# A third w_out block moved out of the big weight transfer, by GpSimd transfers of three shares

## The chip, the core and the metric

The kernel runs on one NeuronCore of a Trainium2 chip. The core has five engines with their own instruction queues: TensorE (PE) multiplies matrices, VectorE (DVE), ScalarE (ACT) and GpSimd (POOL) work on vectors, and SyncE (SP) here only issues DMA transfers. Data comes from HBM into SBUF, a memory of 128 partitions, over 16 DMA engines. The metric is the device time of one execution in microseconds: the kernel before takes 680.47 us (median of three runs, 680.44 to 680.62).

## What is computed

One decoding step of a layer: attention with a key/value cache, and a gated MLP whose output gates the attention's. Cut to what matters:

```python
# x [8,1,512]; k_cache, v_cache [8 batches, 8 kv heads, 4096 keys, 128]; wq [512,4096]; wo [4096,512]
# w_in [512, 1792]; w_out [896, 512]; all float32
xn = layernorm(x)
q  = (xn @ wq) in 32 heads; 4 query heads share one kv head
s  = softmax(q @ k.T / sqrt(128)) @ v, heads joined, @ wo
z  = gelu(xn @ w_in); z1, z2 = z[:896], layernorm(z[896:])
g  = silu((z1 * (w_sp * z2 + b_sp)) @ w_out)
out = x + s * g
```

Almost all bytes are the two caches, 134 MB each. Every byte is used once.

## The kernel before

**Slots.** SBUF holds a ring of three slots of 64 KB per partition (8 MB each). `slot()` takes the next one; a transfer into it waits until the last readers of its old contents are done. The first slot gets wq, the second (`mlp_slot`) all that the MLP needs, the third the first half of K of head 0; from then on K and V halves of the heads follow one another through the ring, each an 8 MB transfer over all 128 partitions, issued by SP in program order (L325 in `load_k`, L332 in `load_v`). At the end come wo and the last V in smaller pieces (L359 to L363), so that little work is left when the last piece lands.

**The MLP's slot.** `w_mlp` is one transfer over 128 partitions (L96): w_in, five of the seven 128-row blocks of w_out, and `side` (x and two scalars). Blocks 1 and 3 of w_out (`MOVED = 2`) are not in it. They lie in `w_ex`, a tile of 64 partitions by 7 units of 512 columns, cleared by a memset on POOL (L98) and then filled by four transfers from SP (L99 and L100). `LANES` lists them: partition group, number of shares of four partitions, first unit, number of units. The four bring 5, 5, 3 and 3 shares; the host lays each array out with a fifth row behind every four (`QUAD + 1`), so that the share stays the leading count of the transfer.

**The MLP's order.** `project_q(0)`, `project_q(1)` and `mlp()` run on PE before the first scores (L347 to L349). In `mlp()`, after gelu and the layer norm, the gated hidden values stand in `u_sb`, 32 rows for each of four column groups. Two transposes make `hT` (L204 to L207) for the five blocks that stayed. For the moved ones `spread` (cleared on POOL, L210) takes the hidden columns in the order in which `w_ex` holds the rows of w_out, by copies that `lane_runs()` lists (L211 to L214); seven transposes give `te`, one copy `hE` (L215 to L219). Then five block matmuls (L224) and seven unit matmuls with 64 rows each (L228) add up in `pw`. The slot is free for V of head 0 when they are done. A scheduler places the instructions of each engine; an instruction that is ready early, such as a memset on POOL, can come ahead of others that stand before it in the program.

**Setup.** POOL also makes the identity (L104), clears `xnT`, `qz`, `pick` and others, and computes the power in the layer norm of x (L149), which all PE work waits for.

Of the kernel before, what the change touches and what calls it, by code (L numbers as in the profile page):

```python
# [8 lines left out]
F32 = mybir.dt.float32  # L9
# [4 lines left out]
P = 128  # L14
B, D = 8, 512
HKV, REP, S, DH = 8, 4, 4096, 128
NK = D // P
G = 4
J = S // (G * P)
R = 32  # L20
FH = 896
FQ = 256
NB = FH // P
MOVED = 2
QUAD = 4
UNITS = 7
LANES = [(0, 5, 0, 6), (1, 5, 0, 5), (1, 3, 5, 2), (0, 3, 6, 1)]
EPS = 1e-5
GELU_C = 0.7978845608028654
HALF = B // 2  # L30
# [7 lines left out]
AHEAD = FOLDED + 2  # L38


def lane_runs():
    f = 0
    for e, k, u, n in LANES:
        m = k * QUAD
        at, end = f, f + n * m
        while at < end:
            g = at // P
            stop = min(end, (g + 1) * P)
            unit, lo = divmod(at - f, m)
            if lo or stop - at < m:  # L50
                whole, size = 1, min(m - lo, stop - at)
            else:
                whole, size = (stop - at) // m, m
            yield g, at - g * P, u + unit, whole, e * R + lo, size
            at += whole * size
        f = end


@with_exitstack
def tile_gqa_gmlp_decode(ctx: ExitStack, tc: tile.TileContext, x, kT, v, wq, wo, w_mlp, w_ex0, w_ex1, w_ex2, w_ex3, out, gate, stored):  # L60
    nc = tc.nc
    head = ctx.enter_context(tc.tile_pool(name="head", bufs=1))
    l = head.tile([P, HKV], F32, name="l")
# [6 lines left out]
    small = ctx.enter_context(tc.tile_pool(name="small", bufs=2))  # L70
# [3 lines left out]
    def slot():  # L74
        return ring.tile([P, SLOT], F32, name="slot")
# [5 lines left out]
    mlp_slot = slot()  # L81
    n_in, n_out = NK * 2 * FH, (NB - MOVED) * D
    n_mlp = n_in + n_out + P
    w_in_sb = mlp_slot[:, :n_in].rearrange("p (k n) -> p k n", k=NK)
    w_out_sb = mlp_slot[:, n_in:n_in + n_out].rearrange("p (j d) -> p j d", j=NB - MOVED)
    side_sb = mlp_slot[:, n_in + n_out:n_mlp]
    spare = [n_mlp]

    def from_slot(rows, n):
        lo = spare[0]  # L90
        spare[0] = lo + n
        return mlp_slot[:rows, lo:lo + n]
# [1 line left out]
    x_sb = from_slot(B, D)  # L94
    nc.sync.dma_start(x_sb, x)
    nc.sync.dma_start(mlp_slot[:, :n_mlp], w_mlp)  # L96
    w_ex = from_slot(2 * R, UNITS * D).rearrange("p (u d) -> p u d", u=UNITS)
    nc.gpsimd.memset(w_ex, 0.0)  # L98
    for (e, k, u, n), src in zip(LANES, (w_ex0, w_ex1, w_ex2, w_ex3)):  # L99
        nc.sync.dma_start(w_ex[e * R:e * R + k * QUAD, u:u + n], src[:, :QUAD])  # L100


    ident = const.tile([P, P], F32, name="ident")
# [30 lines left out]
    def scratch(shape, name):  # L134
        t = ps.tile([P, 512], F32, name="scr")
        n = 1
        for s in shape[1:]:
            n *= s
        return t[:shape[0], :n]
# [18 lines left out]
    def mlp():  # L158
        zu = work.tile([P, 2, 2, FQ], F32, name="zu", tag="p")
        z, u_sb = zu[:, 0], zu[:, 1]  # L160
        rest = work.tile([P, 2 * D], F32, name="rest", tag="pT")
        hT, y_sb = rest[:, :2 * P], rest[:, D:]
        hT = hT.rearrange("p (a s) -> p a s", a=2)
        pz = scratch([P, 2 * FQ], "pz")
        nc.vector.memset(pz, 0.0)
        pz_v = pz.rearrange("p (a f) -> p a f", a=2)
        w_in_v = w_in_sb.rearrange("p k (a f) -> p k a f", a=2)
        for k in range(NK):
            for g in range(G):
                lo = g * FQ  # L170
                n = min(FQ, FH - lo)
                nc.tensor.matmul(pz_v[R * g:R * (g + 1), :, :n], xnT[:, k, :],
                                 w_in_v[:, k, :, lo:lo + n], start=(k == 0), stop=(k == NK - 1))
        zf, uf = z.rearrange("p a f -> p (a f)"), u_sb.rearrange("p a f -> p (a f)")
        nc.vector.tensor_copy(zf, pz)
        nc.vector.tensor_mul(uf, zf, zf)
        nc.vector.tensor_scalar(uf, uf, 0.044715, 1.0, op0=ALU.mult, op1=ALU.add)
        nc.vector.tensor_mul(uf, uf, zf)
        nc.scalar.activation(uf, uf, AF.Tanh, scale=GELU_C)
        nc.vector.tensor_scalar(uf, uf, 1.0, 0.5, op0=ALU.add, op1=ALU.mult)  # L180
        nc.vector.tensor_mul(zf, uf, zf)

        def mean(src, name, eps=0.0):
            part_sum = small.tile([P, 1], F32, name="part_sum")
            nc.vector.tensor_reduce(part_sum, src, op=ALU.add, axis=AX.X)  # L185
            pm = scratch([P, 1], "pm")
            nc.tensor.matmul(pm, same_all, part_sum, start=True, stop=True)  # L187
            t = small.tile([P, 1], F32, name=name)
            nc.vector.tensor_scalar(t, pm, 1.0 / FH, eps, op0=ALU.mult, op1=ALU.add)
            return t  # L190

        z1, z2 = z[:, 0, :], z[:, 1, :]
        mu = mean(z2, "mu")
        nc.vector.tensor_scalar(z2, z2, mu, None, op0=ALU.subtract)
        nc.vector.tensor_mul(u_sb[:, 0, :], z2, z2)
        nc.vector.memset(u_sb[(G - 1) * R:, 0, FH - (G - 1) * FQ:], 0.0)
        var = mean(u_sb[:, 0, :], "var", EPS)
        rs = small.tile([P, 1], F32, name="rs")
        nc.gpsimd.tensor_tensor(rs, var, neg_half, op=ALU.pow)
        nc.vector.tensor_scalar(z2, z2, rs, None, op0=ALU.mult)  # L200
        nc.vector.tensor_scalar(z2, z2, side_sb[:, W:W + 1], side_sb[:, W + 1:W + 2],
                                op0=ALU.mult, op1=ALU.add)
        nc.vector.tensor_mul(u_sb[:, 1, :], z2, z1)
        for a in range(2):  # L204
            th = scratch([P, P], "th")
            nc.tensor.transpose(th, u_sb[:, 1, a * P:(a + 1) * P], ident)  # L206
            nc.vector.tensor_copy(hT[:, a, :], th)  # L207
        wide = MOVED * R
        spread = from_slot(wide, UNITS * 2 * R).rearrange("p (u s) -> p u s", u=UNITS)
        nc.gpsimd.memset(spread, 0.0)  # L210
        for g, f, u, n, lo, m in lane_runs():  # L211
            rows = slice(R * g, R * (g + 1))
            nc.vector.tensor_copy(spread[rows, u:u + n, lo:lo + m],
                                  u_sb[rows, 1, P + f:P + f + n * m].rearrange("p (u s) -> p u s", u=n))  # L214
        te = scratch([2 * R, UNITS * wide], "te")  # L215
        for i in range(UNITS):
            nc.tensor.transpose(te[:, i * wide:(i + 1) * wide], spread[:, i, :], ident[:wide, :wide])  # L217
        hE = from_slot(2 * R, UNITS * wide)
        nc.vector.tensor_copy(hE, te)  # L219
        pw = scratch([P, D], "pw")  # L220
        kept = [j for j in range(NB) if j % 2 == 0 or j // 2 >= MOVED]
        for i, j in enumerate(kept):
            g, a = divmod(j, 2)
            nc.tensor.matmul(pw[R * g:R * (g + 1), :], hT[:, a, R * g:R * (g + 1)], w_out_sb[:, i, :],  # L224
                             start=(a == 0), stop=False)
        for i in range(UNITS):
            lo = wide * (i % 2)
            nc.tensor.matmul(pw[lo:lo + wide, :], hE[:, i * wide:(i + 1) * wide], w_ex[:, i, :],  # L228
                             start=False, stop=(i >= UNITS - 2))
        nc.vector.tensor_copy(y_sb, pw)  # L230
        py = scratch([P, W], "py")
        for g in range(G):
            for a in range(2):
                nc.tensor.matmul(py[R * g:R * (g + 1), :], pick[:, a, :],
                                 y_sb[:, (2 * g + a) * W:(2 * g + a + 1) * W], start=(a == 0), stop=(a == 1))
        nc.vector.tensor_copy(x_out, side_sb[:, :W])
        e = work.tile([P, W], F32, name="e", tag="o_all")
        nc.vector.tensor_scalar(e, py, -1.0, 87.0, op0=ALU.mult, op1=ALU.min)
        nc.scalar.activation(e, e, AF.Exp)
        nc.vector.tensor_scalar(e, e, 1.0, None, op0=ALU.add)  # L240
        nc.vector.reciprocal(e, e)
        nc.vector.tensor_mul(gate, py, e)
# [57 lines left out]
    turn = [0]  # L300
# [34 lines left out]
    part = sc[:, 0, :]  # L335
# [11 lines left out]
    project_q(0)  # L347
    project_q(1)
    mlp()  # L349
    for h in range(HKV):  # L350
        for half in range(2):
# [3 lines left out]
        for half in range(2):  # L355
# [11 lines left out]
            n = 2 if last else HALF  # L367
# [28 lines left out]
    for a in range(2):  # L396
        for g in range(G):
            c = (2 * g + a) * W
            nc.tensor.matmul(acc[R * g:R * g + OUT_ROWS, :], pick[:, a, :OUT_ROWS], part_f[:, c:c + W],
                             start=False, stop=False)  # L400
# [54 lines left out]
```

## Time and profile before

| | |
|---|---|
| median of three runs | 680.47 us (680.44 to 680.62) |
| the profiled execution | 680.28 us |
| its span, first to last instruction | 678.8 us |
| PE, DVE, ACT, POOL busy | 51%, 12%, 2%, 1% |
| DMA | 291 MB, mean 429 GB/s |
| memset of w_ex (L98) | 3.08 us, from 0.88 us |
| x landed (L146 starts) | 22.66 us |
| MLP's last matmul, V of head 0 issued | 63.98 us |
| last piece of wo landed (L391 starts) | 676.25 us |

The profiled execution has 1.48 us around its span. The page gives for each engine its busy time, in forty equal slices the busy tenths of the engines and of the 16 DMA engines together, the DMA queues with their packets (q1 is SP's, q10 the store's from ACT, q8 and q14 are listed as instruction queues), and the chain of waits that ended last. A packet is what one DMA engine moves in one piece, at most 64 KB. Each transfer also leaves one record of 4 bytes per engine that it used, its completion. The time of one packet can be read from a stretch that holds only that packet: its share of 16 engines, times the length of the stretch, times 16.

### The profile page before, as it was taken

What the parts mean: (1) busy time and instruction counts of PE and PEld (TensorE: products, weight loads), DVE (VectorE), ACT (ScalarE), POOL (GpSimd) and SP (SyncE); (2) the same over time, 40 slices, a digit from 0 to 9 for tenths busy, and PEclk for the clock granted to TensorE, in tenths of its full rate; (3) what the DMA queues carried; (4) which work ended last, traced back from release to release, by engine and by line L of the source; (5) the groups of instructions that cost most, each with busy time, mean ns of one, the idle gap of its engine ahead of it and who ended that gap; (6) DMA issues with size and microseconds to landing.
All of it is one profiled execution on the core that took longest, in us unless ns stands there. A gap on an engine that the chain in (4) does not pass through costs nothing.

```text
span 678.8 us, 5218 instructions
## 1 busy us (share of the span) xinstructions
PE 344.0 (51%) x2415; PEld 92.5 (14%) x2415; DVE 83.4 (12%) x159; ACT 13.4 (2%) x27; POOL 7.9 (1%) x17
## 2 busy tenths in 40 slices
PE   0448744446655454555554344555544345555567
PEld 0112211111111011111111011111111011111111
DVE  1143021102110021101100021101101021100221
ACT  0010000000000000000000000000000000000000
POOL 3000000000000000000000000000000000000000
PEclk9987866787776568777666778877666787876679
DMA  9999999999999999999999999999999999999997
GB/s 386 453 441 430 430 433 430 433 430 433 434 433 430 433 433 430 433 441 440 434 433 430 436 436 434 440 434 433 430 433 430 433 433 434 430 436 433 419 427 315
DMA packets 6741, 291.16 MB, mean 429 GB/s; under 512 B 888, under 2 KB 888, under 8 KB 1688
## 3 DMA queue, kind: packets, MB, share of 16 engines
q1 hardware_dynamic: 6576, 290.80, 99.1%
q8 instruction: 19, 0.31, 0.2%
q10 hardware_dynamic: 144, 0.03, 0.0%
q14 instruction: 2, 0.02, 0.0%
HBM read 290.80 MB, written 0.03 MB: 428 GB/s over the span
## 4 chain that ended last, share of the span: by engine, by line
DMA 79%; PE 16%; issue 4%; DVE 0%; SPq 0%; POOLq 0%; POOL 0%
DMA slot<-in_kT 36%; DMA slot<-in_v 33%; PE sc L269 7%; PE o_ps L310 7%; DMA slot<-in_wo 7%; DMA slot<-in_x 3%; PE scr L224 1%; PE scr L228 1%; SPq L332 0%; PE scr L217 0%; DVE st L146 0%; POOLq L449 0%; POOL rstd L149 0%; PE scr L206 0%; PE acc L391 0%
## 5 line engine op out<-in xcount | busy, mean ns | idle before, releaser
L269 PE MATMUL sc<-slot,qz 128*32 128x512 f32 x1024 | 145.4, 731 | 131.2 <-DMA slot<-in_kT 131.2
L310 PE MATMUL o_ps<-slot,pT 128*16 128x512 f32 x1024 | 148.2, 743 | 110.0 <-DMA slot<-in_v 110.0
L269 PEld LDWEIGHTS sc<-slot,qz 128*32 128x32 f32 x1024 | 38.1, 131 | 232.0 <-issue 149.4
L310 PEld LDWEIGHTS o_ps<-slot,pT 128*16 128x16 f32 x1024 | 32.9, 114 | 211.0 <-issue 151.5
L274 DVE TENSOR_REDUCE nm<-sc 128x1 f32<-128x1024 f32 x8 | 9.8, 1225 | 273.7 <-PE sc L269 273.7
L313 DVE TENSOR_TENSOR o_all<-o_ps,diag 128x512 f32<-128x512 f32 x17 | 11.8, 692 | 244.8 <-PE o_ps L310 244.8
L276 ACT ACTIVATE p<-sc,nm 128x1024 f32<-128x1024 f32 x8 | 8.9, 1114 | 551.8 <-DVE nm L274 551.8
L320 PE MATMUL po_ps<-fold,o_sb 128*128 128x16 f32 x30 | 6.0, 274 | 26.8 <-DVE o_sb L315 26.8
L315 DVE TENSOR_REDUCE o_sb<-o_all 128x128 f32<-128x512 f32 x17 | 17.8, 1047 | 0.6
L153 PE MATMUL scr<-ident,slot 8*128 8x8 f32 x4 | 0.6, 254 | 25.0 <-DVE slot L150 25.0
L320 PEld LDWEIGHTS po_ps<-fold,o_sb 128*128 128x128 f32 x30 | 4.5, 189 | 40.6 <-DVE o_sb L315 40.6
L296 DVE STREAM_TRANSPOSE pT<-p 128x1024 f32<-128x1024 f32 x8 | 10.0, 1246 | 0.3
L249 PE MATMUL scr<-slot,xnT 128*32 128x512 f32 x64 | 8.9, 708 | 0.3 <-issue 0.3
L344 PE MATMUL sc<-slot,oT 128*8 128x512 f32 (+1 forms) x60 | 8.4, 565 | 1.1 <-DMA slot<-in_wo 1.0
L279 PE MATMUL scr<-ident,nm 128*1 128x128 f32 x8 | 2.2, 270 | 10.8 <-DVE nm L274 10.8
L292 PE MATMUL scr<-wl,same 128*128 128x1 f32 x16 | 3.6, 297 | 6.5 <-DVE wl L290 6.5
L294 DVE TENSOR_SCALAR p<-p,w,wl 128x1024 f32<-128x1024 f32 x8 | 6.5, 813 | 0.3
L224 PE MATMUL scr<-slot,rest 128*32 128x512 f32 x10 | 5.4, 1044 | 0.0
L187 PE MATMUL scr<-part_sum,same 128*128 128x1 f32 x4 | 1.1, 348 | 8.4 <-DVE part_sum L185 8.4
L285 PE MATMUL scr<-ident,full 1*128 1x1 f32 x8 | 1.8, 220 | 5.0 <-DVE full L283 5.0
L292 PEld LDWEIGHTS scr<-wl,same 128*128 128x128 f32 x16 | 3.2, 249 | 7.0 <-PE scr L285 7.0
L153 PEld LDWEIGHTS scr<-ident,slot 8*128 8x128 f32 x4 | 0.5, 208 | 25.0 <-DVE slot L150 25.0
(94 smaller groups left out, 69.0 us busy)
## 6 DMA issues: line engine op xcount, KB each, us to landing
slot<-in_v SPq DMA_DIRECT2D x2, 4096.0 KB, 28.7
slot<-in_w_mlp SPq DMA_DIRECT2D x1, 4928.0 KB, 32.7
slot<-in_wo SPq DMA_DIRECT2D x1, 2048.0 KB
slot<-in_wo SPq DMA_DIRECT2D x1, 1536.0 KB
slot<-in_wo SPq DMA_DIRECT2D x1, 1280.0 KB, 37.9
slot<-in_wo SPq DMA_DIRECT2D x1, 1024.0 KB
slot<-in_wo SPq DMA_DIRECT2D x4, 256.0 KB, 18.7
slot<-in_wo SPq DMA_DIRECT2D x1, 768.0 KB
```

The source lines that it names most:

```text
L224: nc.tensor.matmul(pw[R * g:R * (g + 1), :], hT[:, a, R * g:R * (g + 1)], w_out_sb[:, i, :], start=(a == 0), stop=False)
L249: nc.tensor.matmul(pq[R * g:R * (g + 1), :], xnT[:, k, :], wq_sb[:, k, lo:lo + REP * DH], start=(k == 0), stop=(k == NK - 1))
L269: nc.tensor.matmul(sc[R * g:R * (g + 1), c, :], qz[:, h, b * R:(b + 1) * R], k_sb[:, i, c, g, :], start=(b == 0), stop=(b == B - 1))
L274: nc.vector.tensor_reduce(m, sc, op=ALU.max, axis=AX.XY, negate=True)
L276: nc.scalar.activation(p, sc.rearrange("p c s -> p (c s)"), AF.Exp, bias=m, accum_out=l[:, h:h + 1])
L292: nc.tensor.matmul(tot, same_all, wl, start=True, stop=True)
L296: nc.vector.transpose(pT.rearrange("p j b g r -> p j g b r"), p.rearrange("p (j g b r) -> p j g b r", j=J, g=G, b=B))
L310: nc.tensor.matmul(of[R * c:R * c + G * REP, :], pT[:, j, b0 + i], v_sb[:, i, j], start=(j < rows), stop=(j >= J - rows))
L313: nc.vector.tensor_mul(o_all, o, diag[:, :, None].to_broadcast([P, G, DH]))
L315: nc.vector.tensor_reduce(o_sb, o_all.rearrange("p g d -> p d g"), op=ALU.add, axis=AX.X)
L320: nc.tensor.matmul(po[:, b0 * REP:(b0 + n) * REP], o_sb, f.rearrange("p i r -> p (i r)"), start=True, stop=True)
L344: nc.tensor.matmul(part[R * q:R * q + B, i * n:(i + 1) * n], oT[:, h, r, :], wo_sb[:, m, i * n:(i + 1) * n], start=(m < REP), stop=(cuts = ...
```

## The change

`MOVED` becomes 3: block 5 of w_out leaves `w_mlp` too, which then holds four blocks. `w_ex` grows from 64 to 128 partitions. The four SP transfers keep their sizes and places. Three more bring the third block: 12 partitions from 84 for units 0 to 4, 12 from 116 for units 0 to 4, and 12 from 84 for unit 6, each of three shares of four partitions. GpSimd issues them (`nc.gpsimd.dma_start`), and ahead of each it issues a transfer of 16 bytes into each of 13 partitions of a small tile `turn`, whose contents nobody reads and of which two buffers exist. `spread` and `hE` become wider: a unit now has 128 rows of w_out, of which the unused ones are zero. `hT` needs only one transpose, as the blocks that stay are the even ones. A fixed list `RUNS` takes the place of `lane_runs()`: eight copies into `spread` instead of six. The host side builds the seven arrays from the same list.

```diff
--- before.py
+++ after.py
@@ -21,10 +21,14 @@
 FH = 896
 FQ = 256
 NB = FH // P
-MOVED = 2
+MOVED = 3
 QUAD = 4
 UNITS = 7
-LANES = [(0, 5, 0, 6), (1, 5, 0, 5), (1, 3, 5, 2), (0, 3, 6, 1)]
+LANES = [(0, 20, 0, 6), (32, 20, 0, 5), (32, 12, 5, 2), (0, 12, 6, 1)]
+HIGH = [(84, 12, 0, 5), (116, 12, 0, 5), (84, 12, 6, 1)]
+RUNS = [(0, 0, 0, 0, 3, 0, 2, 20), (0, 0, 120, 5, 1, 0, 1, 8), (1, 1, 0, 5, 1, 8, 1, 12),
+        (1, 1, 12, 5, 1, 32, 1, 12), (0, 1, 24, 3, 2, 0, 2, 20), (0, 1, 104, 6, 1, 0, 2, 12),
+        (1, 2, 0, 0, 5, 84, 2, 12), (1, 2, 120, 6, 1, 84, 1, 8)]
 EPS = 1e-5
 GELU_C = 0.7978845608028654
 HALF = B // 2
@@ -38,26 +42,8 @@
 AHEAD = FOLDED + 2
 
 
-def lane_runs():
-    f = 0
-    for e, k, u, n in LANES:
-        m = k * QUAD
-        at, end = f, f + n * m
-        while at < end:
-            g = at // P
-            stop = min(end, (g + 1) * P)
-            unit, lo = divmod(at - f, m)
-            if lo or stop - at < m:
-                whole, size = 1, min(m - lo, stop - at)
-            else:
-                whole, size = (stop - at) // m, m
-            yield g, at - g * P, u + unit, whole, e * R + lo, size
-            at += whole * size
-        f = end
-
-
 @with_exitstack
-def tile_gqa_gmlp_decode(ctx: ExitStack, tc: tile.TileContext, x, kT, v, wq, wo, w_mlp, w_ex0, w_ex1, w_ex2, w_ex3, out, gate, stored):
+def tile_gqa_gmlp_decode(ctx: ExitStack, tc: tile.TileContext, x, kT, v, wq, wo, w_mlp, w_ex0, w_ex1, w_ex2, w_ex3, w_hi0, w_hi1, w_hi2, out, gate, stored):
     nc = tc.nc
     head = ctx.enter_context(tc.tile_pool(name="head", bufs=1))
     l = head.tile([P, HKV], F32, name="l")
@@ -94,10 +80,14 @@
     x_sb = from_slot(B, D)
     nc.sync.dma_start(x_sb, x)
     nc.sync.dma_start(mlp_slot[:, :n_mlp], w_mlp)
-    w_ex = from_slot(2 * R, UNITS * D).rearrange("p (u d) -> p u d", u=UNITS)
+    w_ex = from_slot(P, UNITS * D).rearrange("p (u d) -> p u d", u=UNITS)
     nc.gpsimd.memset(w_ex, 0.0)
-    for (e, k, u, n), src in zip(LANES, (w_ex0, w_ex1, w_ex2, w_ex3)):
-        nc.sync.dma_start(w_ex[e * R:e * R + k * QUAD, u:u + n], src[:, :QUAD])
+    for (p, m, u, n), src in zip(LANES, (w_ex0, w_ex1, w_ex2, w_ex3)):
+        nc.sync.dma_start(w_ex[p:p + m, u:u + n], src[:, :QUAD])
+    for (p, m, u, n), src in zip(HIGH, (w_hi0, w_hi1, w_hi2)):
+        turn = small.tile([13, QUAD], F32, name="turn")
+        nc.gpsimd.dma_start(turn, w_mlp[:13, :QUAD])
+        nc.gpsimd.dma_start(w_ex[p:p + m, u:u + n], src[:, :QUAD])
 
 
     ident = const.tile([P, P], F32, name="ident")
@@ -159,8 +149,7 @@
         zu = work.tile([P, 2, 2, FQ], F32, name="zu", tag="p")
         z, u_sb = zu[:, 0], zu[:, 1]
         rest = work.tile([P, 2 * D], F32, name="rest", tag="pT")
-        hT, y_sb = rest[:, :2 * P], rest[:, D:]
-        hT = hT.rearrange("p (a s) -> p a s", a=2)
+        hT, y_sb = rest[:, :P], rest[:, D:]
         pz = scratch([P, 2 * FQ], "pz")
         nc.vector.memset(pz, 0.0)
         pz_v = pz.rearrange("p (a f) -> p a f", a=2)
@@ -201,28 +190,31 @@
         nc.vector.tensor_scalar(z2, z2, side_sb[:, W:W + 1], side_sb[:, W + 1:W + 2],
                                 op0=ALU.mult, op1=ALU.add)
         nc.vector.tensor_mul(u_sb[:, 1, :], z2, z1)
-        for a in range(2):
-            th = scratch([P, P], "th")
-            nc.tensor.transpose(th, u_sb[:, 1, a * P:(a + 1) * P], ident)
-            nc.vector.tensor_copy(hT[:, a, :], th)
-        wide = MOVED * R
-        spread = from_slot(wide, UNITS * 2 * R).rearrange("p (u s) -> p u s", u=UNITS)
+        th = scratch([P, P], "th")
+        nc.tensor.transpose(th, u_sb[:, 1, :P], ident)
+        nc.vector.tensor_copy(hT, th)
+        wide = 2 * R
+        spread = from_slot(wide, UNITS * P).rearrange("p (u s) -> p u s", u=UNITS)
         nc.gpsimd.memset(spread, 0.0)
-        for g, f, u, n, lo, m in lane_runs():
-            rows = slice(R * g, R * (g + 1))
-            nc.vector.tensor_copy(spread[rows, u:u + n, lo:lo + m],
-                                  u_sb[rows, 1, P + f:P + f + n * m].rearrange("p (u s) -> p u s", u=n))
-        te = scratch([2 * R, UNITS * wide], "te")
+        for place, g, f, u, n, p, segs, m in RUNS:
+            dst = spread[place * R:(place + 1) * R, u:u + n]
+            src = u_sb[g * R:(g + 1) * R, 1, P + f:P + f + n * segs * m]
+            if segs == 2:
+                half = p // (2 * R) * 2 * R
+                dst = dst[:, :, half:half + 2 * R].rearrange("p u (e s) -> p u e s", e=2)
+                nc.vector.tensor_copy(dst[:, :, :, p - half:p - half + m],
+                                      src.rearrange("p (u e s) -> p u e s", u=n, e=2))
+            else:
+                nc.vector.tensor_copy(dst[:, :, p:p + m], src.rearrange("p (u s) -> p u s", u=n))
+        te = scratch([P, UNITS * wide], "te")
         for i in range(UNITS):
             nc.tensor.transpose(te[:, i * wide:(i + 1) * wide], spread[:, i, :], ident[:wide, :wide])
-        hE = from_slot(2 * R, UNITS * wide)
+        hE = from_slot(P, UNITS * wide)
         nc.vector.tensor_copy(hE, te)
         pw = scratch([P, D], "pw")
-        kept = [j for j in range(NB) if j % 2 == 0 or j // 2 >= MOVED]
-        for i, j in enumerate(kept):
-            g, a = divmod(j, 2)
-            nc.tensor.matmul(pw[R * g:R * (g + 1), :], hT[:, a, R * g:R * (g + 1)], w_out_sb[:, i, :],
-                             start=(a == 0), stop=False)
+        for g in range(G):
+            nc.tensor.matmul(pw[R * g:R * (g + 1), :], hT[:, R * g:R * (g + 1)], w_out_sb[:, g, :],
+                             start=True, stop=False)
         for i in range(UNITS):
             lo = wide * (i % 2)
             nc.tensor.matmul(pw[lo:lo + wide, :], hE[:, i * wide:(i + 1) * wide], w_ex[:, i, :],
@@ -421,13 +413,18 @@
     vv = c(A_v_cache).reshape(2, HALF, HKV, P, J, G, DH)
     w_out = c(B_w_out).reshape(NB, P, D)
     moved = list(range(1, 2 * MOVED, 2))
-    rows = w_out[moved].reshape(MOVED * P, D)
-    w_ex, f = {}, 0
-    for i, (e, m, u, n) in enumerate(LANES):
-        t = np.zeros((m, QUAD + 1, n, D), np.float32)
-        t[:, :QUAD] = rows[f:f + n * m * QUAD].reshape(n, m, QUAD, D).transpose(1, 2, 0, 3)
-        w_ex[f"w_ex{i}"] = t.reshape(m, QUAD + 1, n * D)
-        f += n * m * QUAD
+    rows = w_out[moved]
+    extra = np.zeros((P, UNITS, D), np.float32)
+    for _, g, f, u, n, p, segs, m in RUNS:
+        part = rows[g, f:f + n * segs * m].reshape(n, segs, m, D)
+        for t in range(segs):
+            extra[p + t * R:p + t * R + m, u:u + n] = part[:, t].transpose(1, 0, 2)
+    w_ex = {}
+    for name, lanes in (("w_ex", LANES), ("w_hi", HIGH)):
+        for i, (p, m, u, n) in enumerate(lanes):
+            t = np.zeros((m // QUAD, QUAD + 1, n * D), np.float32)
+            t[:, :QUAD] = extra[p:p + m, u:u + n].reshape(m // QUAD, QUAD, n * D)
+            w_ex[f"{name}{i}"] = t
     arrays = {
         "x": x,
         "kT": c(k.transpose(2, 0, 7, 1, 5, 3, 6, 4)).reshape(HKV, 2, P, SLOT),
```

## The prediction

> **What bounds the kernel now.** I read the page first: engine shares, DMA row, queues, chain of waits.
>
> ```profile
> span 678.8 us, 5218 instructions
> ...
> DMA  9999999999999999999999999999999999999997
> ...
> q1 hardware_dynamic: 6576, 290.80, 99.1%
> q8 instruction: 19, 0.31, 0.2%
> ...
> q14 instruction: 2, 0.02, 0.0%
> ...
> DMA 79%; PE 16%; issue 4%; DVE 0%; SPq 0%; POOLq 0%; POOL 0%
> ```
>
> The 16 DMA engines are busy in every slice, and nearly all of it is q1, the queue that SP feeds. The 16% of PE in the chain is not a loss: a matmul group releases a slot, SP issues the next load behind transfers that are still running, and the chain runs through the matmuls while the DMA engines work. The chain in order of time shows that, and stretches of the trace (length, then five engines, clock, DMA share, GB/s) show that no engine runs dry until the tail:
>
> ```profile
> 60.32 3.59 PE scr L228 x14
> 63.98 32.31 DMA slot<-in_v
> ...
> 665.08 11.13 DMA slot<-in_wo
> 676.25 0.46 PE acc L391 x16
> ```
>
> ```profile
> 62.00:72.00 10.00, 9.22 (x88) 2.97 (x84) 1.89 (x5) 0.26 (x1) 0.00 (x0) 1.00 1.00 433
> 154.00:628.00 474.00, 240.27 (x1648) 62.72 (x1648) 47.90 (x79) 8.45 (x18) 0.00 (x0) 0.72 1.00 433
> 672.20:674.00 1.80, 1.33 (x14) 0.23 (x14) 0.00 (x0) 0.00 (x0) 0.00 (x0) 1.00 0.84 330
> 674.80:675.60 0.80, 0.69 (x37) 0.47 (x32) 0.29 (x1) 0.00 (x0) 0.00 (x0) 1.00 0.44 172
> 676.00:678.80 2.80, 0.45 (x20) 0.24 (x16) 0.45 (x2) 0.00 (x0) 0.00 (x0) 0.83 0.08 18
> ```
>
> The tail is the heart of it. A share of 0.84 is 13 engines of 16 (0.81, and a little overlap of records); 0.44 is 7. So three engines are done by 672.2, six more between 674.0 and 674.8, and the last seven near 676.1, when the last piece of wo lets L391 go. The seven most loaded engines set the end; the early three have some 3.9 us to spare. What counts is the load of each engine, not the sum.
>
> Where the unevenness comes from shows in the completions (records under 512 B) of the first K load, queued right behind w_ex, counted in 52.7 to 53.3, 56.2 to 56.6 and 56.8 to 57.4 us:
>
> ```profile
> DMA packets 22, 0.72 MB, mean 1202 GB/s; under 512 B 11, under 2 KB 11, under 8 KB 11
> ...
> DMA packets 4, 0.13 MB, mean 328 GB/s; under 512 B 2, under 2 KB 2, under 8 KB 2
> ...
> DMA packets 6, 0.20 MB, mean 328 GB/s; under 512 B 3, under 2 KB 3, under 8 KB 3
> ```
>
> Eleven engines are done first, two 3.4 us later, three 4.4 us later: the w_ex transfers of 5, 5, 3 and 3 shares all start on the same engine. Had each gone on where the last one stopped, 5+5+3+3=16 would have given every engine one share.
>
> **The change, part by part.** Prices of single transfers come from stretches that hold one packet alone, where its time is the share times the stretch times 16. Before this are 16, 10 and 2 KB packets inside q1 (stretches of 6, 5 and 3 ns), then a 64 KB one (10 ns); then a 16 KB instruction fetch of q8 (10 ns) and the q1 packet behind it (20 ns); last an 8 KB packet of q14 (5 ns) and the q1 packet behind it (10 ns):
>
> ```profile
> q1 hardware_dynamic: 1, 0.02, 636.5%
> ...
> q1 hardware_dynamic: 1, 0.01, 481.2%
> ...
> q1 hardware_dynamic: 1, 0.00, 175.0%
> ...
> q1 hardware_dynamic: 1, 0.07, 1511.2%
> ...
> q8 instruction: 1, 0.02, 604.4%
> ...
> q1 hardware_dynamic: 1, 0.07, 901.9%
> ...
> q14 instruction: 1, 0.01, 386.2%
> ...
> q1 hardware_dynamic: 1, 0.07, 1683.8%
> ```
>
> That is 0.611, 0.385, 0.084 and 2.418 us in the queue. The fetch takes 0.967 us where its size costs 0.611, and the q1 packet behind it 2.886 instead of 2.418: a visit of another queue costs that engine 0.36 + 0.47 = 0.82 us over its bytes. The q14 packet takes 0.309 us, which is its bytes' price at (0.611-0.385)/6 KB = 0.0377 us per KB, and the one behind it 2.694: a visit of 0.28 us. These are the two bounds for a visit; q8 has 19 packets, q14 two, and q8's reads are the nearer kind in size, so I take 0.82.
>
> *Less in w_mlp.* Block 5 leaves the 128-partition transfer: 8 rows of 2 KB per engine, 16 KB, 0.60 us less on all sixteen. This is the whole gain; it is on the path.
>
> *The three share transfers.* The first two bring 4 rows of 10 KB to each of three engines, 4x0.385 = 1.54 us; the third 4 rows of 2 KB, 0.34 us; together 3.42 us, plus at least one visit each. Which engines they use, no row shows.
>
> *The three 13-share transfers* (16 B a row) carry no load worth counting, but each is a visit to 13 engines, and 13 of 16 always include at least four of the seven late ones: 3x0.82 = 2.46 us on these.
>
> *GpSimd's queue.* Six issues and a wait of the third 16 B transfer for the first (its tile has two buffers) come ahead of or between the setup work there:
>
> ```profile
> 0.88 3.08 POOL L98 MEMSET slot<- 64x3584 f32 x1
> ...
> 6.87 0.47 POOL L210 MEMSET slot<- 64x448 f32 x1
> ...
> POOL rstd L149 <- DVE rstd L148: 16.5, 1, 16.5
> ...
> 3.98 3.25 SPq L100 DMA_DIRECT2D slot<-in_w_ex  x4
> ```
>
> Behind the wait stand the last share transfer and what the scheduler put after it. No GpSimd issue is in the trace; SP's four cost 0.81 us each, so six are 4.9 us (nothing at the least, and some 10 us if the wait lasts two 64 KB packets), inside the 16.5 us that POOL then idles for L149. The memset of w_ex doubles its partitions, not its 3584 columns: no change. That of spread doubles to 896 columns: 0.5 us, in the same idle time. If that cover went, L149 to L154 and with them q and mlp() would be late; the next cover is below. On SP the four w_ex issues wait for the memset as before, and the first K load's issue stands behind them; were the memset some us later, wq and w_mlp, 13 MB or 31 us of transfers queued ahead, would hide it.
>
> *mlp().* One transpose and copy of hT go, one of five w_out blocks goes, two spread copies come; the unit matmuls use 128 partitions for 64 but the same 512 columns:
>
> ```profile
> 53.08 0.69 PE L206 MATMUL scr<-ident,zu 128*128 128x128 f32 x2 [2.20 <-DVE zu L203]
> ...
> 53.59 0.51 DVE L207 COPY rest<-scr 128x128 f32<-128x128 f32 x2
> ...
> L224 PE MATMUL scr<-slot,rest x10: 897/1060/1061, 54.2 to 59.4; 128*32 128x512 f32 x10
> ...
> L213 DVE COPY slot<-zu x6: 152/162/210, 53.1 to 54.3; 32x12 f32<-32x12 f32 x2, 32x120 f32<-32x120 f32 x1, 32x8 f32<-32x8 f32 x1, 32x80 f32<-32x80 f32 x1
> ```
>
> Roughly -0.35 - 0.26 - 0.9 + 0.32 = -1.2 us, worth nothing: L332 issues V at 63.98 but V lands at 96.29 and needs 8x2.418 = 19.3 us of engine time, so its slowest engine took it up at 76.9 and the quickest 4.4 us sooner: 8.5 us of cover. Only past that would a later mlp() leave an engine idle.
>
> *The sum.* I take one visit per transfer and assume that, as in SP's rows, a 16 B transfer does not shift where the next begins, while the three share transfers follow each other round from the first engines. The first of them then falls on three engines of the 4.4 us group, which are among the late ones: -0.60 + 1.54 + 4x0.82 = +4.2 us. The profiled execution took 680.28 us (span 678.8 and 1.48 outside it), 0.19 under the median of 680.47; the sum is made on it: 684.5 us. Against the ends: 0.28 a visit gives +2.0.
>
> The Trainium skill ("DMA: Bandwidth & Descriptors", section "Why a DMA increments its semaphore by 16 and not by 1") says that a GpSimd transfer on fewer than 16 engines takes consecutive ones from a cursor that moves on, but that some direct copies go out as 16 shares with the partitions spread one by one, which would leave the cursor where it was; by its first half alone the shares would reach the last three engines, which may be the early ones (rivals 2 and 3), by the second not. The trace of before has no such transfer. The same page ("Queues, rings and completion order") has an engine drain a packet of several descriptors before it changes queue; by that rival 4 would not happen; the trace of before cannot show it.
>
> **Rivals.**
> 1. *Everything starts on the same engine,* as SP's transfers do: -0.60 + 3.42 + 6x0.82 = +7.7, 688.0 us. For it: the completions 11, 2, 3. Against: another queue hands these out.
> 2. *The shares reach the three early engines, a visit costs 0.82:* late engines -0.60 + 2.46 = +1.9; the early ones -3.9 - 0.60 + 3.42 + 2.46 = +1.4 against the old end. 682.1 us.
> 3. *The other side, not slower: same place, cheap visits.* At 0.28 or less: -0.60 to +0.2 us, 679.7 to 680.5. For it: the q14 row, and the engines' 3.9 us to spare, which 3.42 - 0.60 fits. Against: q8's row. It decides below 0.20 us a visit for a gain; up to 0.65 it stays within the 0.2%.
> 4. *Each row is a visit of its own,* q1 taking 64 KB between: with my place -0.60 + 1.54 + 7x0.82 = +6.7, 687.0; on the early engines -3.9 - 0.60 + 3.42 + 12x0.82 = +8.8, 689.0 us.
>
> **How the numbers follow.** Forecast 0.32; rival 1 0.07; rival 2 0.14; rival 3 0.15; rival 4 0.16 and 0.11; the rest 0.05, mostly my place with cheap visits, +0.9 to +2.0. The bound of 0.2%, 1.36 us, is about what a measurement of this kernel can tell from no change. Faster by more than it would need more than the 0.60 us that leaves the path: 0.02. Within it: rival 3, the low part of the rest and of rival 2: 0.20. Slower: 0.78. The range 680.1 to 688.8 leaves out the dearest case and most of the cheapest, about 0.2 together; the forecast's own, from 0.28 to 0.82 a visit, is 682.3 to 684.5.
>
> **What would show it.** A new queue row with some 50 data packets of GpSimd. Packets of 10 KB on it taking about 0.74 rather than 0.385 us, and q1 packets near 2.9 us in the first 20 us, would carry the visit; 2.4 would refute it. The share at the tail says the place: still 0.81 for some 4 us or longer if the early engines got nothing, near 1.00 until the end if they did. The completions of the first K load would show a group 1 to 4 us behind the present 57.4. mlp() done after 72 us, or L149 much later than 23.8, would mean that I costed a cover wrongly. Most likely to be wrong: the place of the shares, then the price of a 16 B visit, which no row shows.

## The result and the profile after

The changed kernel takes 684.88 us (median of six runs, 684.67 to 685.31) where the kernel before takes 680.55 beside it (680.29 to 680.74): a ratio of 1.0064, interval 1.0051 to 1.0077, so 4.3 us slower. The profiled execution took 684.86 us, 4.58 more than that of before.

The page of the changed kernel, the lines that answer to those of before:

```profile
span 683.3 us, 5226 instructions
...
q1 hardware_dynamic: 6576, 290.54, 98.9%
q8 instruction: 19, 0.31, 0.2%
q0 software_dynamic: 304, 0.27, 0.1%
...
DMA 79%; PE 16%; issue 4%; DVE 1%; SPq 0%; POOLq 0%; POOL 0%
```

q0 is GpSimd's queue. It moves next to nothing, 0.1% of the engines' time, and the chain has the same shares as before: the loss is in no engine's column. It stands in the completions of the first K load, counted as before, here in 55.70 to 56.35, 57.2 to 57.3, 60.4 to 60.7 and 61.5 to 61.8 us:

```profile
DMA packets 22, 0.79 MB, mean 1210 GB/s; under 512 B 10, under 2 KB 10, under 8 KB 10
...
DMA packets 2, 0.07 MB, mean 655 GB/s; under 512 B 1, under 2 KB 1, under 8 KB 1
...
DMA packets 6, 0.26 MB, mean 874 GB/s; under 512 B 2, under 2 KB 2, under 8 KB 2
...
DMA packets 6, 0.20 MB, mean 655 GB/s; under 512 B 3, under 2 KB 3, under 8 KB 3
```

Ten engines are done 3.0 us later than the eleven of before (they had 0.60 us less to load, so they lost 3.6), one a further 1 us later, and the last five 4.3 to 4.5 us later than their two groups of before. So there are two parts: something that holds up all 16 engines by 3.6 us, and another 1.0 to 1.5 us on six of them, five of which were late already. All of it is there before 62 us; from then on the two executions run alike. The stretches of the tail show groups of three, six and seven engines as before, each later:

```profile
675.40:677.20 1.80, 1.07 (x11) 0.11 (x6) 0.00 (x0) 0.00 (x0) 0.00 (x0) 1.00 0.85 338
678.20:679.40 1.20, 1.02 (x24) 0.37 (x24) 0.53 (x1) 0.00 (x0) 0.00 (x0) 1.00 0.45 172
680.75:683.30 2.55, 0.42 (x16) 0.24 (x16) 0.45 (x2) 0.00 (x0) 0.00 (x0) 0.95 0.06 13
```

Thirteen engines at work, then seven; the last piece of wo lands at 680.7 instead of 676.2.

Single packets of the changed kernel, in stretches of 10 ns (17.03 us), 20 ns (19.44 us) and 7 ns (23.995 us):

```profile
q0 software_dynamic: 2, 0.01, 246.2%
...
q1 hardware_dynamic: 1, 0.07, 890.0%
...
q0 software_dynamic: 1, 0.01, 668.8%
```

The first holds a 10 KB row of a share and a 4-byte packet, which start within the same 10 ns: 0.394 us together, 0.385 and 0.009. So this row took no longer than its bytes take within q1. The second is a 64 KB packet of wq: 2.848 us instead of 2.418. The third is a 10 KB row that took 0.749 us. Such slow packets, of wq and then of w_mlp, stand on all 16 engines from 16.9 us until the last 10 KB row is through at 30.4, and again beside the 2 KB rows until 39.3, although a share transfer has rows on three engines only.

POOL's work shows no loss that counts. In the timeline of its engine:

```profile
1.95 3.11 POOL L84 MEMSET slot<- 128x3584 f32 x1
4.98 0.55 POOL L89 DMA_DIRECT2D turn<-in_w_mlp  x1
5.53 1.14 POOL L90 DMA_DIRECT2D slot<-in_w_hi  x2
10.73 0.53 POOL L89 DMA_DIRECT2D turn<-in_w_mlp  x1 [4.06 <-DMA turn<-in_w_mlp]
...
14.92 0.84 POOL L198 MEMSET slot<- 64x896 f32 x1
```

The scheduler put the small transfers first, so not each share transfer stands behind one. POOL waits 4.06 us for a buffer of `turn` and is done by 15.8 us; x lands at 26.4.

### The profile page after: what moved, and what is told of

The parts are those of the page before. It is cut to its first block, busy times and chain, and to the rows that moved or that the text cites. A ratio compares the mean times of both kernels' runs of the same rounds, so it can differ in the third digit from the quotient of the medians.

```text
span 683.3 us, 5226 instructions
## 1 busy us (share of the span) xinstructions
PE 344.1 (50%) x2412; PEld 92.6 (14%) x2412; DVE 83.2 (12%) x160; ACT 13.4 (2%) x27; POOL 11.8 (2%) x23
## 4 chain that ended last, share of the span: by engine, by line
DMA 79%; PE 16%; issue 4%; DVE 1%; SPq 0%; POOLq 0%; POOL 0%
DMA slot<-in_kT 35%; DMA slot<-in_v 33%; PE o_ps L302 7%; DMA slot<-in_wo 7%; PE sc L261 7%; DMA slot<-in_x 4%; PE scr L220 1%; PE scr L216 0%; PE scr L211 0%; DVE slot L205 0%; DVE st L136 0%; SPq L324 0%; POOLq L446 0%; POOL rstd L139 0%; DVE slot L208 0%
## 5 line engine op out<-in xcount | busy, mean ns | idle before, releaser
L305 DVE TENSOR_TENSOR o_all<-o_ps,diag 128x512 f32<-128x512 f32 x17 | 11.8, 692 | 246.8 <-PE o_ps L302 246.8
L312 PE MATMUL po_ps<-fold,o_sb 128*128 128x16 f32 x30 | 6.0, 276 | 26.4 <-DVE o_sb L307 26.4
L220 PE MATMUL scr<-slot 128*64 128x512 f32 x14 | 5.2, 846 | 0.0
```

The costliest lines, as they stand in the source:

```text
L305: nc.vector.tensor_mul(o_all, o, diag[:, :, None].to_broadcast([P, G, DH]))
L312: nc.tensor.matmul(po[:, b0 * REP:(b0 + n) * REP], o_sb, f.rearrange("p i r -> p (i r)"), start=True, stop=True)
```

## The experiments

Each kernel is the changed one but for its edit. Every time is a median beside its own runs of the kernel before (680.45 to 680.55 us). In the first four expectations the forecast's own reading V, that visits of another queue are dear, is told against two others: R, read from the trace above (the cost comes with the share transfers and falls on all engines), and N (the first four rounds on an engine are free, later ones cost).

**1. The small transfers alone.**

```diff
-    for (p, m, u, n), src in zip(HIGH, (w_hi0, w_hi1, w_hi2)):
+    for _ in HIGH:
         turn = small.tile([13, QUAD], F32, name="turn")
         nc.gpsimd.dma_start(turn, w_mlp[:13, :QUAD])
-        nc.gpsimd.dma_start(w_ex[p:p + m, u:u + n], src[:, :QUAD])
```

> Leaves out the three share transfers (block 5 of w_out then counts as zero); the three 13-row transfers of 16 bytes stay. Theory V (the prediction's): every GpSimd transfer is a visit of 0.82 us on each engine it uses, so -0.60 + 3 x 0.82 = +1.9 us against before, about 682.2 us profiled. Theory R (read from the trace of the changed kernel): the 16-byte rounds are free and the cost comes with the rounds of the share transfers: -0.60 us, about 679.7. Theory N: the first four GpSimd rounds are free on an engine and each later one costs, whatever it carries: six rounds, so -0.60 plus 0.3 to 0.6 us, about 680.1.

679.96 us, ratio 0.9991 (0.9982 to 1.0000). The 0.54 us less are near the 0.60 of block 5, as R has it (V has 1.9 us more, N at most 0.3 less); three small transfers, 96 packets on q0, cost nothing that shows. A visit of a small packet is not dear.

**2. The share transfers alone,** without the three small ones.

```diff
-        turn = small.tile([13, QUAD], F32, name="turn")
-        nc.gpsimd.dma_start(turn, w_mlp[:13, :QUAD])
```

> Leaves out the three 13-row transfers; the share transfers stay, so the whole result is computed. V: -0.60 + 1.54 + 0.82 = +1.8 us on the first three engines, 682.1. R: as in the changed kernel, +4.4 us, 684.7, and the tail shows the same engines late. N: 13 rounds of which the first four are free: +2.5 to +3.5 us, 682.8 to 683.8.

684.67 us, ratio 1.0059 (1.0042 to 1.0075): the changed kernel's time, as R has it; V and N, 682.1 and up to 683.8, fall. The first K load is complete at 55.6 to 57.0 us on ten engines and at 61.6 on the last, as there, so the shares land on the same engines: the small transfers neither cost anything nor moved the place.

**3. Tiny shares:** the same transfers with 16 bytes a row.

```diff
-        nc.gpsimd.dma_start(w_ex[p:p + m, u:u + n], src[:, :QUAD])
+        nc.gpsimd.dma_start(w_ex[p:p + m, u:u + 1, :QUAD], src[:, :QUAD, :QUAD])
```

> The share transfers keep their shape of 3 shares of 4 rows, but a row has 16 bytes instead of 10 or 2 KB (block 5 is then mostly left out). V: as the changed kernel less 1.54 us: 683.0 to 683.4. R, if the rounds themselves cost: also +2.9 us, 683.2. R, if the 10 KB rows cost and the rounds do not: -0.60 us, 679.7. N: 19 rounds, like the changed kernel less 1.54: 683.2.

680.19 us, ratio 0.9993 (0.9984 to 1.0002). With the same six transfers and next to no bytes the cost is gone. There are fewer packets too, though:

```profile
q0 software_dynamic: 192, 0.00, 0.0%
```

instead of 304, because the four 16-byte rows of a share went as one packet of 64 bytes. So this run alone doesn't tell the bytes from the number of visits; experiment 5, with all the rows and 304 packets, does.

**4. The shares on the last three engines.** Each small transfer is 13 rows of two 16-byte pieces and keeps its place ahead of its share transfer, which is held in order by the same call.

```diff
 ...
-        turn = small.tile([13, QUAD], F32, name="turn")
-        nc.gpsimd.dma_start(turn, w_mlp[:13, :QUAD])
+        turn = head.tile([13, 2, 2 * QUAD], F32, name=f"turn{i}")
+        pair = w_mlp[:13, :4 * QUAD].rearrange("p (a q) -> p a q", a=2)
+        t = nc.gpsimd.dma_start(turn[:, :, :QUAD], pair[:, :, :QUAD])
+        tc.keep_in_program_order(t)
 ...
```

> The 13-row transfers become 13 rows of two pieces, so that no single run of rows counts them, and GpSimd's order is held to one of these ahead of each share transfer; the result is complete. If a transfer of 13 shares then moves the place by 13, all share rows land on the three engines that were early: V: late engines -0.60 + 2.46, 682.1. R with costs on all engines in every share round: -0.60 + 3.5 = +2.9 us, 683.2, and the share of busy engines in the tail near 1.0 until some 4 us later than before. If the place does not move: as the changed kernel, 684.7.

683.70 us, ratio 1.0049 (1.0034 to 1.0064). That is near R's 683.2, but not for R's reason: the hold-up of all engines was gone with the same bytes on q0. Completions of the first K load, in 52.10 to 52.85 and in 56.9 to 57.4 us, stand where engines without such rows stood before the change, or up to 0.6 us sooner:

```profile
DMA packets 18, 0.66 MB, mean 874 GB/s; under 512 B 8, under 2 KB 8, under 8 KB 8
...
DMA packets 9, 0.39 MB, mean 786 GB/s; under 512 B 3, under 2 KB 3, under 8 KB 3
```

And yet the end was 3 us late, though at 57.4 us every engine was done with this load, as in the kernel before. Two questions followed: why do rows on engines 0 to 8 hold up all engines and rows on the last three not, and what makes the last three late.

**5 to 7. Engine and partitions, one at a time.** The rows go to partitions 84 to 95 and 116 to 127. Which engine writes these in the 128-partition transfers no row says; the Trainium skill ("SBUF — State Buffer", section "Door 1: The DMA port swizzle") has sets of eight partitions, each behind one port served by one engine, and by it these are engines 13 to 15, and 20 to 31 with 52 to 63 are engines 5 to 7. A row that an engine writes into its own sets is called own here, any other foreign; in the changed kernel all share rows are foreign. So two places of the engines were crossed with two of the partitions. `mid_own` has engines 5 to 7 and their own partitions, `mid_foreign` engines 5 to 7 and partitions of 13 to 15, `last_foreign` engines 13 to 15 and partitions of 5 to 7.

```diff
 # all three: the loop of experiment 4, with its 13 as k; mid_own and mid_foreign with
+        k = 13 if i else 5      # rows of the small transfer
 # mid_own and last_foreign:
-HIGH = [(84, 12, 0, 5), (116, 12, 0, 5), (84, 12, 6, 1)]
+HIGH = [(20, 12, 0, 5), (52, 12, 0, 5), (20, 12, 6, 1)]
-        (1, 2, 0, 0, 5, 84, 2, 12), (1, 2, 120, 6, 1, 84, 1, 8)]
+        (1, 2, 0, 0, 5, 20, 2, 12), (1, 2, 120, 6, 1, 20, 1, 8)]
```

> The same 39 rows of the same sizes, in GpSimd transfers of three shares each; the small transfers ahead of them are 5, 13 and 13 rows of two 16 B pieces, which bring all three shares to engines 5 to 7, and the rows go to partitions 20 to 31 and 52 to 63, which the 128-partition transfers write from engines 5 to 7 themselves. Theory P (partitions: what slows the first K load's neighbours on all 16 engines is that a 10 KB row is written by another engine than the one that writes its partitions in the big transfers; the three foreign groups of partitions take 4 x 22 KB more, 3.4 us, and all engines wait): no slow q1 packets, under 0.3 us of extra time per engine. Theory E (the three early engines of before are 5, 6 and 7, which no instruction fetch reaches): the 3.42 us fit into their 3.9 us, so the end is 0.60 us before that of before: 679.9 us, completions of the first K load near 52.2 (8), 55.8 (5) and 56.7 (3). Rival S (the slow packets come from the three share transfers running on nine engines): the same. Rival to E, the fetches reach 5 to 7 too: their lag of 3.4 grows by two or three fetches of 1.4, 681.7 to 683.7 us.

> As mid_own, on engines 5 to 7, but the rows go to partitions 84 to 95 and 116 to 127 as in the changed kernel, which the big transfers write from engines 13 to 15. Theory P: all engines' q1 packets lose about 3.3 us as in the changed kernel; with engines 5 to 7 the early ones, the end is -0.60 + 3.3 = +2.7: 683.2 us. Rival S: no slow packets, 679.9 us, the same as mid_own.

> As last_engines (13 rows of two pieces each time, all three shares on the last three engines, measured 683.7 us with 0.23 us of extra time per engine), but the rows go to partitions 20 to 31 and 52 to 63, which the big transfers write from engines 5 to 7. Theory P: about 3.3 us of extra time on every engine, 683.7 + 3.1 = 686.8 us. Rival S: no slow packets, 683.7 us.

| | own partitions | foreign partitions |
|---|---|---|
| engines 5 to 7 | 683.58 (683.44 to 685.16) | 687.74 (687.03 to 688.52) |
| engines 13 to 15 | 683.70 (683.48 to 685.21) | 688.52 (687.19 to 688.71) |

Foreign partitions cost 3.4 to 3.7 us between like ends of the ranges, on either engines. (The medians lie 4.2 and 4.8 apart; each range holds two groups 1.5 us apart, for a reason that follows.) The first completions of the first K load, `mid_own` in 52.2 to 52.8 us:

```profile
DMA packets 17, 0.59 MB, mean 983 GB/s; under 512 B 8, under 2 KB 8, under 8 KB 8
```

and `mid_foreign` in 55.8 to 56.6 us:

```profile
DMA packets 16, 0.52 MB, mean 655 GB/s; under 512 B 8, under 2 KB 8, under 8 KB 8
```

The eight engines that move no share are 3.6 to 3.9 us later. Both kernels have as many packets on GpSimd's queue as the changed one:

```profile
q0 software_dynamic: 304, 0.27, 0.1%
```

so the number of visits is not what costs. One 64 KB packet near 17.3 us says how; `mid_own`, 10 ns:

```profile
q1 hardware_dynamic: 1, 0.07, 1511.2%
```

`mid_foreign`, 15 ns:

```profile
q1 hardware_dynamic: 1, 0.07, 1186.7%
```

2.418 us against 2.848: with foreign rows a 64 KB packet on any engine takes some 0.43 us longer while 10 KB rows are under way; with own rows, here and in experiment 4, none of those between 7 and 58 us takes more than 2.454. Theory P's mechanism stands, rival S falls. Its times, 683.2 and 686.8 us, were too low: the first was built on theory E, which fell, and the second is near only the quickest execution, 687.19. The Trainium skill ("SBUF — State Buffer", section "SBUF: two separate sides") names contention at these ports because several engines may write to them; that every engine waits, those with other sets too, it doesn't say.

On the other question theory E fell, which had 679.9 us; its rival, fetches on engines 5 to 7 too, had 681.7 to 683.7. Theory E took 5, 6 and 7 for the three early engines; the tail of `mid_own` has two early engines, and at its end two late ones, then one:

```profile
673.50:675.40 1.90, 1.69 (x15) 0.71 (x18) 0.61 (x3) 0.00 (x0) 0.00 (x0) 1.00 0.90 349
677.60:678.90 1.30, 1.12 (x14) 0.12 (x8) 0.00 (x0) 0.00 (x0) 0.00 (x0) 1.00 0.11 41
679.30:680.70 1.40, 1.23 (x64) 0.76 (x52) 0.45 (x1) 0.00 (x0) 0.00 (x0) 1.00 0.05 19
```

0.90 is 14 engines of 16 and a little overlap, 0.11 about two, 0.05 about one. (In experiment 4 the same stretches have 0.90, 0.13 and 0.06.) By the landings of the loads that one engine is 3.6 to 3.7 us behind the earliest in the first K load, 5.3 after the fetch at 72.9 us, 6.8 after that at 371.9 and 8.3 after that at 659.0. The second of these steps, in 367.05 to 367.10 us (the last completion of one load), 371.90 to 371.95 (the fetch) and 387.95 to 388.05 (the last completion of the next load):

```profile
DMA packets 2, 0.07 MB, mean 1311 GB/s; under 512 B 1, under 2 KB 1, under 8 KB 1
...
q8 instruction: 1, 0.02, 127.2%
...
DMA packets 5, 0.26 MB, mean 2621 GB/s; under 512 B 1, under 2 KB 1, under 8 KB 1
```

The two completions are 20.9 us apart, where 8x2.418 = 19.3 is the time of a load's packets on one engine. These three fetches are the 2nd, 10th and 18th of the 19 packets of q8. Three fetches eight apart on one engine: the packets of 16 KB go round eight engines, then, and an engine gets two or three of them, 1.4 to 1.6 us each. In `mid_foreign` the two late engines get the 6th and 14th and the 7th and 15th, and are 6.5 us behind: where the round begins differs, and one fetch more or less on the last engine would be the 1.5 us between the two groups of times (only one execution of each kernel has a trace). That explains the tail of before: 0 to 4 are late by their w_ex shares (3.3 to 4.4 us), eight engines by fetches (two, 2.8 to 3.2 us, or three, 4.0 and more), and three are early because they get neither. They aren't three neighbours: of 5 to 7 in `mid_own` and of 13 to 15 in experiment 4 two each fell behind by fetches. That instructions are fetched in blocks of 16 KB, 256 to a block, is what the Trainium skill says ("Runtime: NRT & Kernel Launch", section "Instruction fetch mechanics"). The 2412 matmuls with as many weight loads make 18.8 such blocks, which agrees with 19 packets if these are PE's.

**8. The shares by SP,** behind its own four, no small transfers, partitions as in the changed kernel.

```diff
-        nc.gpsimd.dma_start(w_ex[p:p + m, u:u + n], src[:, :QUAD])
+        nc.sync.dma_start(w_ex[p:p + m, u:u + n], src[:, :QUAD])
```

> The three share transfers of the changed kernel issued by SP behind the four of w_ex, without the small transfers; partitions 84 to 95 and 116 to 127 as in the changed kernel. All of SP's transfers start on the first engine, so engines 0 to 2 carry all of it, 3.42 us, and no other queue is in play. Theory P: besides that all engines lose about 3.3 us: -0.60 + 3.42 + 3.3 = +6.1, 686.6 us. Rival S, and a rival by which the slow packets belong to GpSimd's queue: -0.60 + 3.42 = +2.8, 683.3 us.

686.57 us, ratio 1.0089 (1.0075 to 1.0102), the time that theory P gave. The hold-up isn't GpSimd's: SP's rows into foreign partitions do it as well. SP's own four w_ex transfers are the counterpart: they go to partitions 0 to 19 and 32 to 51, by the mapping above those of engines 0 to 4 that write them, and in the kernel before no 64 KB packet beside them takes more than 2.427 us. P's split was not what the trace shows, though. Completions of the first K load, 58.30 to 59.60 and 63.15 to 63.50 us:

```profile
DMA packets 31, 1.07 MB, mean 826 GB/s; under 512 B 13, under 2 KB 13, under 8 KB 13
...
DMA packets 11, 0.52 MB, mean 1498 GB/s; under 512 B 3, under 2 KB 3, under 8 KB 3
```

Engines 0 to 2 are where P put them, 6.2 us later than before; but the other thirteen, of which P had eleven at 55.6, are at 58.3 or later, held up by some 6 us. So the time came out although P's split did not. SP's rows follow one another without 64 KB packets between; whether that is why they cost more was not tried.

**9 and 10. What a foreign row costs.** Three transfers of three rows, by engines 0 to 2, each into three sets of partitions or into one. The two entries of block 5 in `RUNS` go as well.

```diff
-    for (p, m, u, n), src in zip(HIGH, (w_hi0, w_hi1, w_hi2)):
 ...
+    for i, p in enumerate((84, 116, 72)):       # three_ports; one_port: p:p + 3
+        t = nc.gpsimd.dma_start(w_ex[p:p + 12:4, 0:5],
+                                w_hi0[:, i].rearrange("s (u d) -> s u d", u=5))
```

> Instead of the six GpSimd transfers of the changed kernel three of three rows of 10 KB each, by engines 0 to 2, a row per engine; within a transfer the rows go to partitions 4 apart (84, 88, 92; 116, 120, 124; 72, 76, 80), which in the big transfers belong to three different engines. Block 5 is left out of the output. Theory P1 (what all engines wait for is the one set of eight partitions that gets more than its share, so a transfer's rows cost the bytes that fall on the busiest set): 10 KB a transfer, 0.385 to 0.43 us, 1.2 to 1.3 us in all; completions of the first K load on the engines without rows near 52.75 - 0.60 + 1.25 = 53.4. Theory P2 (every foreign row costs its own time, one after the other): 9 rows x 0.385 = 3.5 us, near 55.6. End: engines 0 to 2 carry 1.15 us of rows, -0.60 + 1.15 + 1.25 = +1.8 by P1, 682.3 us; +4.0 by P2, 684.5 us.

> As three_ports, the same nine rows of the same sizes by the same engines, but within a transfer they go to neighbouring partitions (84 to 86; 116 to 118; 72 to 74), which in the big transfers all belong to one engine. Block 5 is left out of the output. Theory P1: 30 KB a transfer on one set of eight partitions, 1.15 to 1.3 us each, 3.5 to 3.9 in all; completions of the first K load on the engines without rows near 55.7, end -0.60 + 1.15 + 3.5 = +4.0, 684.5 us. Theory P2: the same as in three_ports, 684.5 us too. A third, P0 (each foreign row delays only by its own 0.385 and the rows of a transfer run side by side whatever their partitions): 53.4 and 682.3 us in both.

`three_ports` took 682.02 us, ratio 1.0023 (1.0014 to 1.0033), `one_port` 683.30, ratio 1.0042 (1.0025 to 1.0059). Nine rows, one after the other, would have cost 3.5 us in both: P2 falls. First completions in `three_ports`, 53.10 to 53.85 us:

```profile
DMA packets 20, 0.66 MB, mean 874 GB/s; under 512 B 10, under 2 KB 10, under 8 KB 10
```

in `one_port`, 53.35 to 53.95 and 54.30 to 55.35 us:

```profile
DMA packets 16, 0.52 MB, mean 874 GB/s; under 512 B 8, under 2 KB 8, under 8 KB 8
...
DMA packets 11, 0.52 MB, mean 499 GB/s; under 512 B 3, under 2 KB 3, under 8 KB 3
```

Beside experiment 1, where eleven engines are done at 52.3 to 52.6, most engines lose 0.9 to 1.4 us in either kernel, about three times the 0.385 us of a row. So P1 too is right only for three sets: rows that run at once delay most engines by the time of one, even into one set, as P0 has it. Into one set three engines lose 1.8 to 2.7 us (into three sets one engine 2.1), and the end comes 1.3 us later, which P0 does not explain.

## Why the prediction was right, and where it was not

**The time.** 684.5 us was forecast, 684.88 measured; by the profiled execution +4.2 against +4.58. The sum was right, and one of its three terms, the largest, had the right size for a wrong reason.

**Less in w_mlp, -0.60.** Right: -0.54 in experiment 1.

**The share, +1.54 on late engines, and the place.** Right. The 16-byte transfer doesn't shift where the next begins, and the three share transfers go round from the first engine: last five completions 4.3 to 4.5 us later, the ten engines without a 10 KB share 3.0; the difference, 1.3 to 1.5, is the term forecast at 1.54. Of the Trainium skill's passage that the prediction cites on the place, the second half was the one that held; by the first the shares would have been on the last three engines, and experiment 4 shows that these are not the early ones, so rivals 2 and 3 would have failed there too, by the fetches on two of them.

**Four visits of 0.82, +3.28.** This step failed. The visits cost nothing that shows (experiment 1, and experiment 5 with 304 packets on q0 and no slow 64 KB packet). What stands in their place is 3.3 to 3.7 us on every engine, because the rows are written into partitions of another engine (experiments 5 to 8). The q8 row from which the 0.82 came was a true price of a fetch, but the nearest in size wasn't the nearest in kind; the 0.28 of the q14 row was closer, and still too high. That the two sums agree to 0.4 us is chance: with own partitions and the same place the sum would have been about +0.9.

**What was to show it.** The q1 packets near 2.9 us came (2.848), and a 10 KB packet of 0.749; both were meant as marks of visits, and foreign rows make the same marks. A count of such packets on engines that have no rows to move would have told the two apart. The Trainium skill's sentence, cited in the prediction, that an engine drains several descriptors before it changes queue was not borne out for the 10 KB rows: those of one share start at 17.03, 19.96 and 23.51 us on an engine, with a 64 KB packet of q1 between. For shorter rows it agrees with the trace: the 2 KB rows went two to a packet (six packets of 4 KB), the 16-byte rows of experiment 3 four. Rival 4 was right in that each 10 KB row is a visit of its own, and wrong in its price.

**The covers.** All held. POOL still idled 11.8 us before L139, the power in the layer norm, and mlp() ended at 67.33 instead of 63.98 us, in the changed kernel's chain:

```profile
62.08 5.19 PE scr L220 x14
67.33 33.42 DMA slot<-in_v
```

The 3.35 us come from x, which landed 3.7 us later in the held-up queue, and are inside the 8.5 us of cover.

**The other side.** Faster was given 0.02. The experiments show why there was little to win even with the right place and the right partitions: the 3.9 us to spare are those of three engines that aren't neighbours, and every other engine has either shares or fetches. If they are the same three in every kernel, one is among 5 to 7, one among 13 to 15 and one among 8 to 12; which ones stays open. A kernel with the shares on just these three was not tried, and the 0.60 us it could gain is less than the 1.36 us that the prediction takes for the least a measurement tells. No complete version that beats the kernel before came out of this.

## What to carry to other kernels

Where all DMA engines are busy, a transfer that one engine writes into partitions that another engine writes in the big transfers is paid by all engines: here by 3.3 to 3.7 us where 64 KB packets stood between the rows, about as long as the share rows take three at a time (3.42 us), and by some 6 us where none did. Lay the data out so that each share goes to its engine's own partitions, and it costs only that engine (experiments 4 and 5). Before giving work to engines that look idle at the end, ask what made the others late: here instruction fetches that go round eight engines. And when a trace offers two prices for an unseen event, 0.28 and 0.82 us here, look for a mark that only one mechanism leaves, since a right sum doesn't prove its terms.

## What was not expected

- Foreign rows slow the 64 KB packets of all 16 engines from 2.418 to 2.848 us, also of engines that neither send nor own such rows. Why all of them wait wasn't settled.
- A GpSimd transfer of three shares leaves packets of 4 or 8 bytes, 0.009 us each as a rule, on the engines that have no data too: 235 of the 304 packets on q0 in the changed kernel are so small. If each of the six transfers leaves a completion on all 16 engines, 96 of them are completions, and the other 139 stand for engines without data.
- The late tail of a kernel with 19 fetches is set in part by which engines fetch: 1.4 to 1.6 us each time.
